# Loading pairs of KV-cache units as 2 MB transfers with 16 KB runs in a decode kernel

## The chip, the cores and the metric

The kernel runs on one core of one Trainium2 chip; the other cores are idle. The metric is the device time of one execution in microseconds (us), of which the profiled span is some 2 us less. One program differs from run to run (the kernel before gave 638.4 to 641.0 us in all sessions together), so each kernel is compared with runs of the kernel before from the same rounds, with an interval.

## The reference, cut to what matters

Two decoder layers, twice the same pair of blocks: attention of one new token against a KV cache, then a gated feed-forward block. Both layers use the same weights and the same caches.

```python
B, Sq, D = 4, 1, 512
Hq, Hkv, Sk, Dh = 32, 8, 8192, 128          # bf16 everywhere
def _A_ref(x, k_cache, v_cache, wq, wo):     # attention
    q = (x @ wq)...                          # 4 query heads share a KV head
    p = softmax(q k^T * Dh**-0.5);  o = p v
    return o @ wo
x = x + _A_ref(_layernorm(x), ...);  x = x + _B_ref(_layernorm(x), ...)   # layer 1
x = x + _A_ref(_layernorm(x), ...);  x = x + _B_ref(_layernorm(x), ...)   # layer 2
```

For each batch and KV head, K and V are 8192 rows of 256 bytes, 2 MB each: 4 x 8 x 2 x 2 MB = 128 MB a layer. Layer 2's query of a batch needs that batch's whole layer 1 first.

## The kernel before

PE is TensorE, PEld its weight load, DVE VectorE, ACT ScalarE, and SPq the queue of SyncE that issues the loads. The kernel streams the caches as *units* of 1 MB (half of one head's K or V), each into one of 11 *slots* of 8 KB per partition (15 once the query weights are no longer needed). A static *plan* simulates PE, DVE, ACT and the load queue and fixes the order of every instruction before the program is built; a list of tokens, ORDER, gives the order of the loads: `K` is the next key unit, `a061` layer 1's values of batch 0, head 6, half 1, `b...` the same for layer 2. A `c` token loads nothing: it is a value unit of layer 2 that has stayed in its slot since layer 1. The last unit is loaded in two halves, to shorten the tail. (A unit of 1 MB is 2^20 bytes; in lines of the profile and in the curves below, MB are 10^6 bytes.)

```python
class Plan:
    HOP = 0.06
    PAGE = 6.0          # us; the plan's own figure for PAGE_N instructions of PE
    PAGE_N = 256
    LOAD_LEAD = 2.1     # us; the plan's own figure, issue to first byte
    LOAD_TAIL = 1.7     # us; the plan's own figure, last byte to semaphore
...
def load_pair(u):
    kind, l, b, g, cp = u
    def fn():
        s = PL.slot[home[u]]
        cache = A_k_cache if kind == "k" else A_v_cache
        src = cache[b, g, cp * 2 * CR:(cp + 1) * 2 * CR, :].rearrange("(p t) d -> p (t d)", p=P)   # 1 MB, 8 KB per partition
        T.dma("sp", slot_sb(s), src, sem_slot[s], ...)      # waits until the slot's last reader is done
    return PL.load(2.495, fn, u)                            # 2.495 us in the plan; the last unit goes another way
...
def chain(b, deps, prior):                                  # from layer 1's attention of batch b to layer 2's query
    s = add_x(x0T[:], "x0", None, deps)
    opj_free[0] = s
    s = ffn(s, f"f{b}")
    cen, root = layer_norm(s, f"q{b}n")
    ...                                                     # query projection, spread over the key layout
k_order = [(g, cp) for cp in range(NCP) for g in range(G)]  # key units: half 0 of all heads, then half 1
```

Of the kernel before, what the change touches and what calls it, by code (L numbers as in the profile page):

```python
# [100 lines left out]


class Step:
    __slots__ = ("eng", "us", "deps", "fn", "prio", "take", "free", "start", "end", "slot_of", "n", "gives")

    def __init__(self, eng, us, fn, deps, prio, take=None, free=None, n=0):
        self.n = n
        self.eng, self.us, self.fn, self.prio = eng, us, fn, prio
        self.deps = [d for d in deps if d is not None]
        self.take, self.free = take, free  # L110
        self.start = self.end = None
        self.slot_of = None
        self.gives = 0


class Plan:

    HOP = 0.06
    PAGE = 6.0
    PAGE_N = 256  # L120
    LOAD_LEAD = 2.1
    LOAD_TAIL = 1.7

    def __init__(self, nslots, banks):
        self.steps = []
# [7 lines left out]
        self.steps.append(s)  # L133
        return s

    def load(self, us, fn, slots):
        s = Step("sp", us, fn, [], [0])
        s.slot_of = slots
        self.loads.append(s)
        return s  # L140

    def run(self):
# [19 lines left out]
        def finish(s):  # L162
            done.append(s)
            for u in users.get(s, ()):
                waits[u] -= 1
                if waits[u] == 0:
                    t = max(d.end + (self.HOP if d.eng != u.eng else 0.0) for d in u.deps)
                    todo[u.eng].append((t, u))

        def pump(now):  # L170
            nonlocal li, sp_at, dma_at
            while li < len(self.loads):
                s = self.loads[li]
                t = sp_at
                if s.slot_of is not None:
                    if not slots:
                        return
                    slots.sort()
                    f, i = slots[0]
                    t = max(t, f)  # L180
                    if t > now:
                        return
                    slots.pop(0)
                    self.slot[s.slot_of] = i
                s.start = t
                sp_at = t + 0.35
                dma_at = max(dma_at, t + self.LOAD_LEAD) + s.us
                s.end = dma_at + self.LOAD_TAIL
                li += 1
                finish(s)  # L190
# [18 lines left out]
        while left:  # L209
            best = None  # L210
            for e in engines:
                cand = None
                for t, s in todo[e]:
                    if s.take is not None:
                        b = min(bank_free.values()) if bank_free else None
                        if b is None:
                            continue
                        t = max(t, b)
                    at = max(t, free_at[e])
                    k = (at > free_at[e] + 1e-9, at if at > free_at[e] + 1e-9 else 0.0, s.prio[0])  # L220
                    if cand is None or k < cand[0]:
                        cand = (k, at, s)
                if cand is not None and (best is None or cand[1] < best[0]):
                    best = (cand[1], cand[2])
            nxt = None
            if li < len(self.loads) and (slots or self.loads[li].slot_of is None):
                nxt = max(sp_at, min(slots)[0] if self.loads[li].slot_of is not None else 0.0)
            if best is None and nxt is None:
                raise RuntimeError("the plan is stuck")
            if best is None or (nxt is not None and nxt <= best[0]):  # L230
                pump(nxt)
                continue
            at, s = best
            s.start, s.end = at, fetched(at, s)
            free_at[s.eng] = s.end
            for i, (_, x) in enumerate(todo[s.eng]):
                if x is s:
                    todo[s.eng].pop(i)
                    break
            if s.take is not None:  # L240
                b = min(bank_free, key=lambda x: bank_free[x])
                del bank_free[b]
                held[s.take] = b
                self.bank[s.take] = b
            if s.free is not None:
                bank_free[held.pop(s.free)] = s.end + self.HOP
            if s.slot_of is not None:
                slots.append((s.end + self.HOP, self.slot[s.slot_of]))
            for i in range(s.gives):
                slots.append((s.end + self.HOP, self.nslots + i))  # L250
            left -= 1
            finish(s)
# [4 lines left out]
    def emit(self):  # L257
        for s in sorted(self.steps + self.loads, key=lambda s: (s.start, s.prio[0])):
            s.fn()


ORDER = ("c100 c101 K K c260 x K c300 c301 c261 K wq K K wg1 c120 K K c340 K K K K c341 K a061 K K K wo1 a060 "
         "K K wo0 K K a010 K c240 K K a071 c121 a011 wg0 c031 K a070 a000 c370 K c371 a040 a001 K a050 K wu0 "
         "a030 c030 K a041 a051 K K K K a020 K a031 a021 a150 wo2 a151 a171 a170 wo3 wu1 wd0 wd1 a160 a161 "
         "a131 a130 K K K a121 K a110 a111 K K K K K K K K K K K b010 c241 a141 a120 b011 a140 a100 K K K K K "
         "b061 K K K K K K b060 a101 K b070 K K K b071 K c200 c201 b040 b041 b050 b051 b020 b001 b000 b021 K "
         "K K a250 c141 a251 K c140 K K K K K K K K K K K K a270 K a271 a220 a221 a210 a260 a201 K K K K K "
         "a240 K a200 a261 a241 K a230 K a231 K K a211 K b151 b150 K K b160 K b170 K b171 c321 b161 b110 b130 "
         "b131 b111 K a330 a310 K K a360 K K K K K K a361 K K a331 K K K K K a320 a350 a351 a311 a300 a370 "
         "a301 a341 a340 a321 a371 b230 b250 b231 b251 b220 b221 K K K K K K K K K K K K K K K K b210 b271 "  # L270
         "b270 b310 b211 b360 b320 b351 b311 b350 b331 b330 b361 ")
NSLOT = 11
NP = 2
NQB = 1
# [6 lines left out]
def bass_interleave_layers__gqa_block_cached__swiglu_ffn__decode_kernel(  # L281
# [18 lines left out]
    P = 128  # L300
# [14 lines left out]
    with ExitStack() as es:  # L315
# [230 lines left out]
        def slot_sb(s):  # L546
            return pool[:, s, :] if s < NSLOT else wq_sb[:, s - NSLOT, :]

        def load_pair(u):
            kind, l, b, g, cp = u  # L550

            def fn():
                s = PL.slot[home[u]]
                cache = A_k_cache if kind == "k" else A_v_cache
                src = cache[b, g, cp * 2 * CR:(cp + 1) * 2 * CR, :].rearrange("(p t) d -> p (t d)", p=P)
                T.dma("sp", slot_sb(s), src, sem_slot[s],
                      writes=[f"slot{s}_0", f"slot{s}_1"] + ([f"wq{s - NSLOT}"] if s >= NSLOT else []))
            home[u] = u
            if u != last_unit:
                return PL.load(2.495, fn, u)  # L560

            def half(h):
                s = PL.slot[home[u]]
                src = A_v_cache[b, g, cp * 2 * CR:(cp + 1) * 2 * CR, :].rearrange("(p h t) d -> p h (t d)", p=P, h=2)
                T.dma("sp", slot_sb(s)[:, h * UE:(h + 1) * UE], src[:, h, :], sem_half if h == 0 else sem_slot[s],
                      writes=[f"slot{s}_{h}"] + ([f"wq{s - NSLOT}"] if s >= NSLOT and h == 0 else []))
            return [PL.load(1.25, lambda: half(0), u), PL.load(1.25, lambda: half(1), None)]

# [333 lines left out]
            fs = slice(k * FO // 2, (k + 1) * FO // 2)  # L902
            wspec[f"wd{k}"] = (wd_sb[:, fs, :], B_w_down.rearrange("(fo p) n -> p fo n", p=P)[:, fs, :], 2.6)

        k_order = [(g, cp) for cp in range(NCP) for g in range(G)]
        k_order = [x for x in k_order if x[0] >= G // 2] + [x for x in k_order if x[0] < G // 2]

        def k_units(l, b):
# [10 lines left out]
        late_groups = [(1, B - 1, g) for g in LATE]  # L919
        last_unit = None  # L920
        if TAILSPLIT:
            last_unit = ("v", 1) + tuple(int(x) for x in [t for t in tokens if t[0] == "b"][-1][1:])

        w_load = {}
        loads = {}
# [1 line left out]
        ki = 0  # L927
        wq_load = None
        for npos, t in enumerate(tokens):
            if t == "K":  # L930
                u = kseq[ki]
                ki += 1
                prio[u] = [npos]
                if u[1] == 1 and ("k", 0) + u[2:] in kept_k:
                    home[u] = ("k", 0) + u[2:]
                else:
                    loads[u] = load_pair(u)
            elif t[0] in "abc":
                u = ("v", int(t[0] != "a")) + tuple(int(x) for x in t[1:])
                prio[u] = [npos]  # L940
                if t[0] == "c":
                    home[u] = ("v", 0) + u[2:]
                else:
                    loads[u] = load_pair(u)
            elif t == "x":
                x_load = PL.load(0.1, lambda: T.dma("sp", xrow, A_x.rearrange("b s d -> (b s) d"), sem_x,
                                                    writes=["xrow"]), None)
            elif t == "wq":
                wq_load = w_piece(wq_sb[:], A_wq.rearrange("(kt p) n -> p kt n", p=P), "wq", 9.94)
            else:  # L950
                w_load[t] = w_piece(*wspec[t][:2], t, wspec[t][2])
# [120 lines left out]
```

## Time and profile before

| | |
|---|---|
| time | 639.13 us (638.86 to 639.25, 3 runs) |
| span of the profile | 636.9 us |
| bytes loaded by queue 1 | 256.14 MB in 97.9% of the span |
| PE, DVE | 62%, 64% busy |

The prediction below shows the page's own lines. One more view belongs to it: what the issuing queue waits for (columns: who waited for whom; us in total, times, longest).

```profile
SPq L62 <- PE ps L601: 297.0, 112, 12.3
SPq L62 <- PE ps L742: 133.5, 67, 10.4
```

For two thirds of the span the issuer waits for PE to finish with a slot (L601 are the key matmuls, L742 the value matmuls). That is harmless as long as enough loads are already queued (queue 1 is busy for 97.9% of the span all the same).

### The profile page before, as it was taken

Reading aid. Unit: us, or ns where it says so; the run is one execution under the profiler, and the core shown is the slowest. Engines: PE = TensorE matmul, PEld = TensorE weight load, DVE = VectorE, ACT = ScalarE, POOL = GpSimd, SP = SyncE. Lnnn points to the kernel's source line nnn. Section 1 sums busy time; section 2 is a strip of 40 time slices with the busy share of each in tenths; the row PEclk is TensorE's granted clock in tenths of the full one; section 3 lists DMA queues with packets and bytes.
Section 4 is the critical chain, followed back from the end, with each engine's and each line's share of the span. In section 5 each row is a group of like instructions: output and inputs, shape, how many; then the busy total and the mean of one; then the engine's idle time right before and its main releaser. Section 6 shows DMA issues by size and latency. Waiting matters only on the chain.

```text
span 636.9 us, 18667 instructions
## 1 busy us (share of the span) xinstructions
PE 397.2 (62%) x8689; PEld 201.8 (32%) x8689; DVE 405.1 (64%) x615; ACT 40.4 (6%) x107; POOL 1.8 (0%) x8
## 2 busy tenths in 40 slices
PE   0375454365685556668577665668666676867576
PEld 0231221123552132235331241333421244621255
DVE  6386853464236958776578866457667863499832
ACT  1000200002000020000100100000100020000200
POOL 1000000000000000000000000000000000000000
PEclk9995586556557775655665687655566568576785
DMA  8999999999989999999999999999999999999991
GB/s 359 419 419 406 407 417 420 418 419 403 387 355 422 420 421 418 420 419 402 413 412 419 421 419 420 421 420 397 421 420 419 418 409 420 419 416 420 420 417 68
DMA packets 41125, 257.33 MB, mean 404 GB/s; under 512 B 3924, under 2 KB 9816, under 8 KB 11096
## 3 DMA queue, kind: packets, MB, share of 16 engines
q1 hardware_dynamic: 41048, 256.14, 97.9%
q8 instruction: 68, 1.11, 0.7%
q14 instruction: 9, 0.07, 0.0%
HBM read 256.12 MB, written 0.00 MB: 402 GB/s over the span
## 4 chain that ended last, share of the span: by engine, by line
DMA 66%; PE 15%; DVE 12%; SPq 3%; issue 2%
DMA pool<-in_A_k_cache_dram 44%; DMA pool<-in_A_v_cache_dram 13%; DVE pool L585 10%; PE ps L601 8%; DMA wq_sb<-in_A_v_cache_dram 5%; DMA wq_sb<-in_A_k_cache_dram 4%; PE ps L742 3%; SPq L92 3%; PE ps L463 1%; PE ps L788 1%; DVE wq_sb L585 1%; DVE ps L769 0%; PE ps L852 0%; PE ps L727 0%; PE ps L705 0%
## 5 line engine op out<-in xcount | busy, mean ns | idle before, releaser
L585 DVE STREAM_TRANSPOSE pool<-pool 128x2048 uint32<-128x2048 uint32 x116 | 266.9, 2308 | 91.3 <-DMA pool<-in_A_k_cache_dram 90.8
L601 PE MATMUL ps<-pool,qpad 32*32 32x512 bf16 x3840 | 193.2, 537 | 128.3 <-DVE pool L585 124.7
L601 PEld LDWEIGHTS ps<-pool,qpad 32*32 32x32 bf16 x3840 | 54.8, 108 | 243.9 <-DVE pool L585 184.4
L742 PE MATMUL ps<-pool,pp 128*32 128x256 bf16 x1936 | 98.8, 359 | 46.7 <-DMA pool<-in_A_v_cache_dram 36.5
L742 PEld LDWEIGHTS ps<-pool,pp 128*32 128x32 bf16 x1936 | 55.3, 118 | 82.8 <-DMA pool<-in_A_v_cache_dram 42.1
L769 DVE STREAM_TRANSPOSE ps<-ps 128x256 f32<-128x256 f32 x62 | 28.3, 457 | 60.9 <-PE ps L742 60.6
L624 ACT ACTIVATE pp<-ps,negm 128x512 bf16<-128x512 f32 x32 | 21.5, 685 | 322.3 <-DVE negm L620 299.8
L705 PE MATMUL ps<-oT,wo_sb 128*128 128x4 bf16 x640 | 22.6, 166 | 12.0 <-DVE oT L773 9.4
L705 PEld LDWEIGHTS ps<-oT,wo_sb 128*128 128x128 bf16 x640 | 20.2, 103 | 24.6 <-DVE oT L773 17.8
L620 DVE TENSOR_REDUCE negm<-ps 128x1 f32<-128x512 f32 x32 | 19.9, 683 | 11.6 <-PE ps L601 11.6
L463 PE MATMUL ps<-xnT,wq_sb 128*128 128x4 bf16 x640 | 18.3, 166 | 12.8 <-DMA wq_sb<-in_A_wq_dram 11.4
L463 PEld LDWEIGHTS ps<-xnT,wq_sb 128*128 128x128 bf16 x640 | 17.7, 104 | 15.2 <-DMA wq_sb<-in_A_wq_dram 11.6
L585 DVE STREAM_TRANSPOSE wq_sb<-wq_sb 128x2048 uint32<-128x2048 uint32 x8 | 18.5, 2311 | 1.3 <-DMA wq_sb<-in_A_k_cache_dram 1.3
L449 ACT ACTIVATE lnv<-var,eps_sb 128x4 f32<-128x4 f32 x10 | 3.0, 298 | 221.3 <-DVE var L444 221.3
L601 PE MATMUL ps<-wq_sb,qpad 32*32 32x512 bf16 x256 | 12.3, 512 | 7.4 <-DVE wq_sb L585 7.4
L660 PE MATMUL ps<-ident,pp 128*128 128x128 bf16 x128 | 15.8, 301 | 1.6 <-DVE oT L773 1.1
L660 PEld LDWEIGHTS ps<-ident,pp 128*128 128x128 bf16 x128 | 12.0, 138 | 9.1 <-DVE selw L680 2.9
L771 DVE TENSOR_REDUCE osum<-ps 128x4 f32<-128x32 f32 x62 | 11.9, 192 | 2.1
L773 DVE TENSOR_TENSOR oT<-osum,invL 128x4 bf16<-128x4 f32 x62 | 10.5, 169 | 2.1
L669 ACT ACTIVATE pp<-ps 128x1024 bf16<-128x1024 bf16 x8 | 8.2, 1023 | 29.7 <-PE ps L660 29.7
L671 DVE COPY pp<-ps 128x1024 bf16<-128x1024 bf16 x8 | 5.5, 690 | 6.8 <-PE ps L660 6.8
L649 DVE TENSOR_SCALAR pp<-pp,alpha 128x512 bf16<-128x512 bf16 x32 | 9.0, 344 | 1.1 <-ACT alpha L642 1.1
(68 smaller groups left out, 150.4 us busy)
## 6 DMA issues: line engine op xcount, KB each, us to landing
pool<-in_A_k_cache_dram SPq DMA_DIRECT2D x116, 1024.0 KB, 10.2
pool<-in_A_v_cache_dram SPq DMA_DIRECT2D x101, 1024.0 KB, 10.7
wq_sb<-in_A_k_cache_dram SPq DMA_DIRECT2D x8, 1024.0 KB, 14.8
wq_sb<-in_A_v_cache_dram SPq DMA_DIRECT2D x5, 1024.0 KB, 16.3
wq_sb<-in_A_wq_dram SPq DMA_DIRECT2D x1, 4096.0 KB, 20.1
wo_sb<-in_A_wo_dram SPq DMA_DIRECT2D x4, 1024.0 KB, 15.2
wg_sb<-in_B_w_gate_dram SPq DMA_DIRECT2D x2, 896.0 KB, 19.2
wu_sb<-in_B_w_up_dram SPq DMA_DIRECT2D x2, 896.0 KB, 16.9
```

Source lines behind the costliest of these rows:

```text
L92: ins = self.eng[engname].dma_start(out_ap, in_ap)
L463: op("pe", lambda e: e.matmul(ps[:, bk * BW + h * B:bk * BW + (h + 1) * B], lhsT=wq_sb[:, kt, h * Dh:(h + 1) * Dh], rhs=xnT[:, kt * B:(kt ...
L585: op("dve", lambda e: e.transpose(v, v), reads=keys, writes=keys)
L601: op("pe", lambda e: e.matmul(ps[32 * c:32 * (c + 1), a * BW:(a + 1) * BW], lhsT=qpad[rows, qbuf, es_, g, :], rhs=ap[h][rows, :, es_ // 2, ...
L620: op("dve", lambda e: e.tensor_reduce(negm[:, q, a:a + 1], bank(a), AX.X, ALU.max, negate=True), reads=[f"pb{a}"], writes=[f"negm{q}_{a}"])
L624: op("act", lambda e: e.activation(pblk(q)[:, :, a, :], bank(a).rearrange("p (t j) -> p t j", j=32), ACTF.Exp, bias=negm[:, q, a:a + 1], s ...
L660: op("pe", lambda e: e.matmul(stg[:, t * P:(t + 1) * P], lhsT=pp[:, q, blk * P:(blk + 1) * P], rhs=ident[:], is_transpose=True, start=True ...
L705: op("pe", lambda e: e.matmul(ps[:, OPJ * BW + nq * B:OPJ * BW + (nq + 1) * B], lhsT=wo_sb[:, h, nq * P:(nq + 1) * P], rhs=oT[:, l, h, :], ...
L742: op("pe", lambda e: e.matmul(ps[32 * n:32 * (n + 1), bk * BW:bk * BW + 256], lhsT=pp[:, q, col:col + 32], rhs=v[:, 8 * f:8 * (f + 1), 32 ...
L769: op("dve", lambda e: e.transpose(blk, blk), reads=[f"pb{bk}"], writes=[f"pb{bk}"])
L771: op("dve", lambda e: e.tensor_reduce(osum[:], diag, AX.X, ALU.add), reads=[f"pb{bk}"], writes=["osum"])
L773: op("dve", lambda e: e.tensor_tensor(oT[:, l, g * REP:(g + 1) * REP, b], got, invL[:, q, g * REP:(g + 1) * REP], ALU.mult), reads=[f"pb{b ...
```

## The change

The intent: fewer, longer packets. Each partition now holds 64 adjacent rows of a head's cache (16 KB) instead of two separate runs of 32, so that both units of a head can come as one 2 MB load of 16 KB runs into two adjacent slots. 27 pairs are loaded so (tokens `P`, `A..`, `B..`); the other units are still singles, which now read 8 KB out of every 16 KB. The plan's constants change too, and the order of the keys.

```diff
-    PAGE = 6.0
+    PAGE = 5.0
-    LOAD_TAIL = 1.7
+    LOAD_TAIL = 2.1
...
+        def rows_of(u):
+            cache = A_k_cache if u[0] == "k" else A_v_cache
+            return cache[u[2], u[3], :, :].rearrange("(p c t) d -> p c (t d)", p=P, c=NCP)
+
+        def load_two(u0, u1):
+            def fn():
+                s = PL.slot[u0]
+                to = pool[:, s:s + 2, :] if s < NSLOT else wq_sb[:, s - NSLOT:s - NSLOT + 2, :]
+                T.dma("sp", to.rearrange("p c e -> p (c e)"), rows_of(u0).rearrange("p c e -> p (c e)"), sem_slot[s], ...)
...
+            return PL.load(4.914, fn, u0, u1)
...
-                src = cache[b, g, cp * 2 * CR:(cp + 1) * 2 * CR, :].rearrange("(p t) d -> p (t d)", p=P)
-                T.dma("sp", slot_sb(s), src, sem_slot[s],
+                T.dma("sp", slot_sb(s), rows_of(u)[:, cp, :], sem_slot[s],
...
-                return PL.load(2.495, fn, u)
+                return PL.load(2.505, fn, u)
...
-        k_order = [(g, cp) for cp in range(NCP) for g in range(G)]
+        k_order = [(g, cp) for g in range(G) for cp in range(NCP)]
... (the scheduler learns to wait for two adjacent free slots; ORDER gets 16 P, 7 A and 4 B tokens)
```

## The prediction

> **What bounds the kernel now.** I read the page first, for the engine shares, the slices and the DMA queues.
>
> ```profile
> PE 397.2 (62%) x8689; PEld 201.8 (32%) x8689; DVE 405.1 (64%) x615; ACT 40.4 (6%) x107; POOL 1.8 (0%) x8
> DMA  8999999999989999999999999999999999999991
> GB/s 359 419 419 406 407 417 420 418 419 403 387 355 422 420 421 418 420 419 402 413 412 419 421 419 420 421 420 397 421 420 419 418 409 420 419 416 420 420 417 68
> DMA packets 41125, 257.33 MB, mean 404 GB/s; under 512 B 3924, under 2 KB 9816, under 8 KB 11096
> q1 hardware_dynamic: 41048, 256.14, 97.9%
> q8 instruction: 68, 1.11, 0.7%
> DMA 66%; PE 15%; DVE 12%; SPq 3%; issue 2%
> ```
>
> No compute engine is busy for two thirds of the span, while queue 1 is busy for 97.9% of it and moves about 420 GB/s in most slices. The last line, from the chain that ended last, agrees: 66% of it is DMA. So the kernel lasts as long as 256.14 MB take, plus a start, a tail, and the places where the queue runs dry. Those I looked for with the windows view in stretches of 5 us (columns: stretch, length, busy time and count of PE, PEld, DVE, ACT, POOL, then clock, DMA share, GB/s), and with the timeline of the issuing queue.
>
> ```profile
> 180.00:185.00 5.00, 3.99 (x158) 3.65 (x163) 0.91 (x5) 0.31 (x2) 0.00 (x0) 0.50 1.01 418
> 185.00:190.00 5.00, 4.58 (x108) 1.92 (x93) 3.30 (x5) 0.00 (x0) 0.00 (x0) 0.69 0.62 223
> 190.00:195.00 5.00, 3.60 (x138) 2.28 (x135) 0.00 (x0) 0.00 (x0) 0.00 (x0) 1.00 1.01 421
> ...
> 620.00:625.00 5.00, 1.87 (x67) 1.77 (x64) 0.83 (x3) 0.00 (x0) 0.00 (x0) 0.50 0.69 283
> 625.00:630.00 5.00, 3.77 (x114) 3.47 (x112) 1.28 (x8) 0.00 (x0) 0.00 (x0) 0.50 0.04 10
> ```
>
> ```profile
> 177.52 10.20 SPq L92 DMA_DIRECT2D pool<-in_A_v_cache_dram  x2
> 188.35 10.90 SPq L92 DMA_DIRECT2D pool<-in_A_k_cache_dram  x9
> ```
>
> The one real dry spell is at 185 to 190: 223 instead of 420 GB/s loses (1 - 223/420) x 5 = 2.3 us. The timeline says why: between the two loads of the group that begins at 177.52 and the nine of 188.35 the issuer sat for some 10 us, because the slots are full of layer 2's keys, which cannot be used before layer 2's query of batch 0 (its projection runs at 179.56 to 183.6 in the chain). Other soft stretches lose less: 393 and 385 at 285 to 295 are 0.3 + 0.4 us, 395 at 325 is 0.3, 380 at 435 is 0.5. The slices with 403, 387 and the rest of the loss in 355 (slices 10 to 12) hold the weights in 1 KB and 3.5 KB runs, not a wait. After the stream has ended near 625 a tail of about 12 us runs on PE and DVE: last value group, output projection, feed-forward.
>
> [...] its packet records give a median of 159 ns for 4096 B and 312 ns for 8192 B (most frequent 309), so 4096 B more cost 150 to 153 ns, 26.8 to 27.3 bytes per ns. [...] In this trace the overhead is what is left at zero size: 159 - 150 = 9 ns; 1024 B take 46 to 48 ns, of which 38 at that rate are data, again 8 to 10 ns. Completion packets of 4 B take 9 ns. [...] The pitch here goes from 8 to 16 KB; no run here shows what that does yet. [...] The 68 instruction packets of 16 KB take a median of 1073 ns beside the stream, where 16 KB alone should take about 610, so they do share; they also show that the trace records 16 KB as one packet.
>
> **The change part by part.** (a) *Bytes: none.* The order before has 235 units of 1 MB to place, less 4 kept keys, so 231 loads (116 + 8 + 101 + 5 whole, and one in two halves). After it are 177 singles and 27 pairs, 177 + 54 = 231; the list of kept values is the same 21. (b) *Packets.* A single is 8 packets of 8 KB on each engine and a completion: 8 x 312 + 9 = 2505 ns. A pair is 8 packets of 16 KB and one completion. My estimate of a 16 KB packet is 2 x (312 - 9) + 9 = 615 ns, so the pair takes 8 x 615 + 9 = 4929 ns against 2 x 2505 = 5010. Saved: 0.081 us a pair, 27 x 0.081 = 2.2 us in all. The constants in the plan (4.914 for a pair, 2.505 for a single) would say 27 x 0.096 = 2.6 us; they are what the author believes, and near mine. As the queue never pauses over most of the span, this should reach the end nearly whole; it also moves the query of batch 0 forward, since that waits for loads in front of it. (c) *Issue.* 27 issues fewer of about 0.35 us, but the queue works at least 10 us ahead (median of issue to landing 10.2 us), so this is worth 0. (d) *Singles with a hole.* The 177 singles now read 8 KB out of every 16 KB. Packets keep their size, so I expect 2.505 us still: 0. (e) *Pairs wait for two adjacent slots and land as one.* 14 of the 27 are in the first 63 MB, when slots come free in order; the others stand in a few stretches (149 to 164 MB and the last 35). The first unit of a pair becomes usable up to 2.4 us later; with some 4 MB always in flight the engines have work meanwhile: 0 to +0.5 us. (f) *New order of loads.* The search had new constants (page time 5, landing tail 2.1). Around the dry spell the tokens are nearly the same as before, with again 11 keys in a row before b010, so I expect most of its 2.3 us to stay: -0.5 us on average. (g) *Tail.* The pair B33 now stands before the last value load; before, its two units did, one of them landing about 2.5 us before the end (its matmuls start at 623.74 and run without a gap). The pair lands in the same place, so the tail stays at 12 us: 0.
>
> Sum: 639.1 - 2.2 (packets) - 0.5 (order) + 0.2 (pairing waits) = 636.6 us.
>
> **The rivals.** *Holes hurt.* If half-covered 16 KB blocks cost the memory something, say 1% of a single (0.025 us), the 177 singles lose 4.4 us and the time goes to 641. [...] Against it: the other half mostly follows within a few loads and the packets are the same. *Two adjacent slots turn into dry spells.* One more spell such as that at 185 costs 2.3 us, so 639; two, 641. For it: the issuer already waits for slots most of the span. Against it: the median 10 us in flight cover most waits, and the plan was made for them. *The new order removes the dry spells.* All of them together are about 4 us; with half gone the time is 634.5, with all near 632.7. Against it: that at 185 hangs on a chain of results, not on packets. [...] *The transfer was at its ceiling anyway*, by reads and not by packets: then (b) gives 0 and the time is 638.5 to 639.
>
> **Range and chances.** The sure part is small, 2.2 us or 0.35%; schedule luck is of the same size, about 2 us each way, and the holes add some weight above. I take 636.6 us, 633.0 to 640.5. Faster by 2% means below 626.3; that is more than the packets and every dry spell together (639.1 - 2.2 - 4 = 632.9), so 2%. Slower by 2% means above 651.9, a loss of over 2.8% on each single, or five more dry spells: 3%. Within 2%: 95%.
>
> **What would show it.** Right: packets fall by 27 x 128 in data and 27 x 16 in completions, to about 41125 - 3888 = 37240; 16 KB packets near 615 ns, 8 KB ones still at 312; clean slices that hold pairs at 425 or so against 420; bytes the same; the dry spell still near 183 to 187; a tail of about 12 us. Wrong: 8 KB packets longer than 314 ns (holes), 16 KB packets at 624 or more (no overhead to save), new stretches under 400 GB/s away from the weights (slots), or the stretch at 185 back at 420 (order).

"Its packet records" are those of the trace of before. Three figures are estimates from the trace of before: the 610 ns of 16 KB alone is 4 x 150 + 9, the 2.4 us of (e) is 4.929 - 2.505, and its 4 MB are 10.2 us at 420 GB/s. The 1% of "holes hurt" is a supposition; nothing measured stood behind it.

## The result, and the profile after

The changed kernel takes 639.02 us (median of 4, 638.6 to 640.06), the kernel before 639.19 us in the same rounds; the ratio is 0.9997, with a 95% interval of 0.998 to 1.0015. (A ratio is the mean time of one kernel's runs over that of the other's in the same rounds, so not quite the ratio of the medians.) The same program ran once more by accident, as x_pair8k below: 0.9989. Together that is 0.2 to 0.7 us of gain instead of the 2.5 us forecast, within noise of nothing.

The page of the changed kernel, the same lines as shown of before:

```profile
PE 397.1 (62%) x8689; PEld 205.1 (32%) x8689; DVE 402.7 (63%) x615; ACT 40.4 (6%) x107; POOL 1.8 (0%) x8
DMA  8999999999989999999999999999999999999991
GB/s 356 423 426 412 405 417 423 420 418 401 387 348 400 422 418 419 420 412 421 402 408 419 422 425 428 417 408 420 418 408 421 415 419 421 417 409 419 423 425 65
DMA packets 37237, 257.32 MB, mean 404 GB/s; under 512 B 3492, under 2 KB 9384, under 8 KB 10664
q1 hardware_dynamic: 37160, 256.14, 97.7%
q8 instruction: 68, 1.11, 0.7%
DMA 63%; PE 18%; DVE 16%; issue 2%; SPq 0%; ACT 0%
```

The packets fell to 37237 as worked out, the bytes are the same, and some slices run at 423 to 428 GB/s. But the busy share of queue 1 fell as well, from 97.9 to 97.7% of a span that is no shorter: time that the packets no longer need has become idle time. Slices 12 and 13 (348, 400; before 355, 422) show where. The windows of the changed kernel there, and at the end, then its issuing queue at the spell:

```profile
185.00:190.00 5.00, 4.02 (x80) 1.69 (x79) 3.13 (x4) 0.00 (x0) 0.00 (x0) 0.50 0.62 215
190.00:195.00 5.00, 4.49 (x160) 2.63 (x144) 0.00 (x0) 0.00 (x0) 0.00 (x0) 0.91 0.96 339
620.00:625.00 5.00, 2.08 (x76) 1.78 (x73) 0.83 (x3) 0.00 (x0) 0.00 (x0) 0.94 0.66 270
625.00:630.00 5.00, 3.78 (x114) 3.48 (x112) 1.28 (x8) 0.00 (x0) 0.00 (x0) 0.50 0.03 9
```

```profile
176.69 10.76 SPq L92 DMA_DIRECT2D pool<-in_A_v_cache_dram  x2
188.13 7.07 SPq L92 DMA_DIRECT2D pool<-in_A_k_cache_dram  x8
```

The dry spell is still at 185 to 190 (215 GB/s, before 223) and goes on into the next stretch, 339 GB/s where before had 421. The issuer stops at 176.69 us, 0.83 us sooner than before (177.52), but goes on with keys at 188.13, only 0.22 us sooner (188.35). The end of the stream is at the same place.

The packet records of the trace give the sizes. The median 16 KB packet took 614 ns (estimate 615), the median 8 KB packet 311 ns (312). All packets of queue 1 together, over 16 engines, come to 622.2 us in the changed kernel and 622.5 in its repetition, against 623.6 and 624.0 in the two profiles of before: about 1.5 us less.

To find where these were lost, I took from the same records the moment by which a given number of MB had been moved. Every kernel here moves the same MB in all, so the difference of two such curves is the time one is ahead. Negative is ahead of the first profile of before:

| | at 75 MB (before: 184.9 us) | at 85 MB (211.1 us) | at 255 MB (620.8 us) |
|---|---|---|---|
| changed kernel | -0.60 | +0.55 | 0.00 |
| the same, repeated (x_pair8k) | -0.79 | +0.80 | -0.19 |

All 14 pairs ahead of the spell are loaded before 66 MB (13 of them before 55), and by 75 MB the changed kernel is 0.6 to 0.8 us ahead. It loses all of it and more within the ten MB that hold the dry spell. From there to the end it wins back 0.5 to 1.0 us.

### The profile page after: what moved, and what is told of

Read it like the earlier page. It is cut to its first block, busy times and chain, and to the rows that moved or that the text cites. A ratio compares the mean times of both kernels' runs of the same rounds, so it can differ in the third digit from the quotient of the medians.

```text
span 636.9 us, 18609 instructions
## 1 busy us (share of the span) xinstructions
PE 397.1 (62%) x8689; PEld 205.1 (32%) x8689; DVE 402.7 (63%) x615; ACT 40.4 (6%) x107; POOL 1.8 (0%) x8
## 2 busy tenths in 40 slices
DMA packets 37237, 257.32 MB, mean 404 GB/s; under 512 B 3492, under 2 KB 9384, under 8 KB 10664
## 3 DMA queue, kind: packets, MB, share of 16 engines
q1 hardware_dynamic: 37160, 256.14, 97.7%
## 4 chain that ended last, share of the span: by engine, by line
DMA 63%; PE 18%; DVE 16%; issue 2%; SPq 0%; ACT 0%
DMA pool<-in_A_k_cache_dram 39%; DMA pool<-in_A_v_cache_dram 18%; DVE pool L606 12%; PE ps L622 7%; PE ps L763 5%; DMA wq_sb<-in_A_wq_dram 3%; PE ps L472 2%; DMA wo_sb<-in_A_wo_dram 2%; DMA wq_sb<-in_A_k_cache_dram 2%; DVE wq_sb L606 1%; PE ps L809 1%; PE ps L726 1%; DVE ps L790 1%; PE ps L681 1%; PE ps L873 1%
## 5 line engine op out<-in xcount | busy, mean ns | idle before, releaser
L622 PE MATMUL ps<-pool,qpad 32*32 32x512 bf16 x3840 | 190.6, 543 | 127.2 <-DVE pool L606 120.7
L763 PEld LDWEIGHTS ps<-pool,pp 128*32 128x32 bf16 x1936 | 57.5, 122 | 81.6 <-DMA pool<-in_A_v_cache_dram 42.8
L472 PE MATMUL ps<-xnT,wq_sb 128*128 128x4 bf16 x640 | 18.3, 166 | 12.1 <-DMA wq_sb<-in_A_wq_dram 11.4
L438 PE MATMUL ps<-xx,onesm 128*128 128x32 f32 x20 | 6.3, 410 | 5.3 <-DVE xx L433 4.3
```

The costliest lines, as they stand in the source:

```text
L472: op("pe", lambda e: e.matmul(ps[:, bk * BW + h * B:bk * BW + (h + 1) * B], lhsT=wq_sb[:, kt, h * Dh:(h + 1) * Dh], rhs=xnT[:, kt * B:(kt ...
L622: op("pe", lambda e: e.matmul(ps[32 * c:32 * (c + 1), a * BW:(a + 1) * BW], lhsT=qpad[rows, qbuf, es_, g, :], rhs=ap[h][rows, :, es_ // 2, ...
L763: op("pe", lambda e: e.matmul(ps[32 * n:32 * (n + 1), bk * BW:bk * BW + 256], lhsT=pp[:, q, col:col + 32], rhs=v[:, 8 * f:8 * (f + 1), 32 ...
```

## The experiments

15 runs. In the tables of "ahead" the numbers are as above.

### The packets by themselves: s_seq, s_hole, s_pair

A program of nothing but loads: 256 MB of the caches into ten slots, no compute.

```diff
 s_seq:  src = [head[c * 4096:(c + 1) * 4096, :].rearrange("(p t) d -> p (t d)", p=P) for c in range(2)]
 s_hole: src = [head.rearrange("(p c t) d -> p c (t d)", p=P, c=2)[:, c, :] for c in range(2)]
 s_pair: src = [head.rearrange("(p t) d -> p (t d)", p=P)]        # two slots at once
```

> The disputed cost by itself: nothing but loads, all 128 MB of K and V caches twice (256 loads of 1 MB), contiguous 1 MB halves as in the kernel before, ten slots, no compute (the result is wrong on purpose). From the packet records of before, a load is 8 x 312 + 9 = 2.505 us, so 256 take 641 us, about 646 us with start and end. Theory (packets cost 9 ns each, holes cost nothing) and its rivals agree on this run; it is the base for the next two.

> The same stream of 1 MB loads, but each load reads 8 KB out of every 16 KB, as the changed kernel's singles do (wrong result on purpose). Theory: equal to s_seq within 1 us, 8 KB packets at a median of 311 to 312 ns. Rival 'holes hurt': 1% or more slower (6 us), 8 KB packets at 315 ns or more.

> The same bytes as 128 loads of 2 MB in 16 KB runs (wrong result on purpose). Theory: a pair is 8 x 614 + 9 = 4.921 us against 5.010, so 128 x 0.089 = 11.4 us less than s_seq (about 1.8%). Rival 'the transfer was at its ceiling anyway': equal to s_seq within 2 us.

Measured: 644.44, 645.05 and 634.0 us (one run each, spans 642.6, 643.2 and 632.2). The pages of s_seq, s_hole and s_pair, in this order:

```profile
DMA packets 36898, 268.47 MB, mean 418 GB/s; under 512 B 4128, under 2 KB 4128, under 8 KB 4128
```

```profile
DMA packets 36898, 268.47 MB, mean 417 GB/s; under 512 B 4128, under 2 KB 4128, under 8 KB 4128
```

```profile
DMA packets 18465, 268.46 MB, mean 425 GB/s; under 512 B 2080, under 2 KB 2080, under 8 KB 2080
```

The pairs save 10.44 us in 128, 0.082 us each, the estimate to within a hundredth (mean 16 KB packet 615.5 ns, mean 8 KB packet 313.8). The holes cost 0.6 us in 256 loads, one run each, and the curves of the two streams stay within 0.12 us of each other. So the packet step of the prediction was right, and "the transfer was at its ceiling anyway" and "holes hurt" are both wrong for a bare stream. (The saving of 11.4 us expected of s_pair was 1 us too high.)

### An attempt that said nothing: x_pair8k

```diff
-T.dma("sp", to.rearrange("p c e -> p (c e)"), rows_of(u0).rearrange("p c e -> p (c e)"), sem_slot[s],
+T.dma("sp", to, rows_of(u0), sem_slot[s],
```

> The changed kernel with the same 27 pairs in the same order, each still one 2 MB load with one completion, but its runs are 8 KB (the two slots are written as separate pieces): 27 x 128 more packets, nothing else. Theory (the packet saving is real, but some of it is lost where the queue is dry anyhow): 0.7 to 2.0 us slower than the changed kernel, so 639.7 to 641, ratio to before 1.001 to 1.003. Rival 'packets are worth nothing here': equal to the changed kernel, ratio 1.000. Note that if the pair is still cut into 16 KB packets the run says nothing; the packet count will show it (40693 or so, against 37237).

It took 638.97 us, ratio 0.9989 (0.9977 to 1.0001). Its page has the packets of the changed kernel and not the 40693 wanted:

```profile
DMA packets 37237, 257.32 MB, mean 404 GB/s; under 512 B 3492, under 2 KB 9384, under 8 KB 10664
```

The two adjacent pieces were loaded as runs of 16 KB again (the record does not show what merged them). The run is therefore a repetition of the changed kernel and is used as that; it tells nothing of packets.

### The parts of the change alone: x_consts, x_korder, x_holes, x_nopairs, and before_again

x_consts is before with `PAGE = 5.0`, `LOAD_TAIL = 2.1` and 2.505 us per single. x_korder adds the new `k_order`. x_nopairs is the changed kernel with the ORDER of before (constants, holes and key order, no pairs); x_holes is that with the key order of before. The plan gives all four the same schedule: their traces have the same instructions in the same order on every engine. All four load in the ORDER of before, so none of them tests the new order.

> The kernel before with only the plan's constants of the change (page time 5, landing tail 2.1, single load 2.505), its own order of loads, no pairs, contiguous halves. It separates what the other schedule costs from what the pairs bring. Theory A (the change's gain from pairs was spent by its schedule): 1 to 2 us slower than before, ratio 1.0015 to 1.003. Theory B (the pairs never brought the gain inside this kernel): equal to before within 0.5 us.

> x_consts with the key units in the change's order (both halves of a head one after the other), contiguous halves, no pairs. x_nopairs was 1.3 us slower than x_consts; it differs by this order and by the holes. If the order of the keys does it: ratio 1.002 or more (640.7). If not: as x_consts, 1.000 (639.4).

> x_nopairs with the key units in the order of before: holes and constants alone. The bare streams say that holes cost under 0.6 us in 256 loads. If they are as cheap here: 639.4 to 640.0, ratio 1.000 to 1.001. If the holes made x_nopairs slow: 640.7 or more, 1.002.

> The changed kernel with the order of loads of before, so no pairs: its layout (64 adjacent rows per partition, singles with holes) and its constants alone. The static schedule of the engines is the same as in x_consts, only the rows that a load brings differ. Theory: equal to x_consts within 0.5 us. Rival 'holes hurt': 231 loads slower by 1% each, 5.8 us more than x_consts. If theory A of x_consts holds, the changed kernel is 1 to 2 us faster than this one.

> The kernel before once more, unchanged: it shows how far two sets of runs of one program differ, and a second profile of the dry spell near 185. In the first profile of before the TensorE clock came back from half to full at 188.1, in all four kernels of the other schedules only at 190.8 to 191.6, so that their slots came free about 1.2 us later. Theory 'luck of the clock': the step to full speed lies anywhere between 187 and 192 in this profile too, and if it is late the dry stretch is as long as in the changed kernel. Theory 'schedule': it lies at 188 again. Ratio 1.000.

| | median us | ratio to before (95%) | ahead at 75, 85, 255 MB |
|---|---|---|---|
| before_again | 639.27 | 0.9998 (0.9986 to 1.001) | -0.08, +0.37, +0.37 |
| x_consts | 639.62 | 1.0003 (0.999 to 1.0016) | -0.14, +0.34, +0.98 |
| x_korder | 639.64 | 1.0003 (0.9991 to 1.0015) | -0.05, +0.42, +1.37 |
| x_holes | 639.90 | 1.0008 (0.9995 to 1.0021) | 0.00, +0.41, +0.62 |
| x_nopairs | 640.89 | 1.0024 (1.0012 to 1.0037) | +0.15, +0.98, +2.21 |

Only x_nopairs is clear of noise, at +1.5 us. Neither of its two layout parts alone shows that, and the bare stream clears the holes, but no run repeats both parts together, so whether its excess over x_holes is chance stays open. x_consts has the time of theory B (equal to before) and not of A (1 to 2 us slower), though its interval reaches A's lower end. What the four have in common is that behind the dry spell they lose 0.2 to 1.2 us (85 to 255 MB, mean 0.8), which the two profiles of before do not, and their ratios average 1.0010, 0.6 us. So the new constants, with the old order of loads, are perhaps half a microsecond worse than the old ones; each single run is too coarse to say more.

before_again also answers its own question in part: the clock came back to full at 189.0 there, against 188.1 in the first profile and 190.8 to 191.6 in the changed kernel, its repetition, the four above and x_early below. It varies within one program, but whether the later step of these seven is chance or schedule stays open. The constants alone do not fix it: the last two kernels below have them too, and there it came at 187.4 and 192.4.

### Only the pairs ahead of the spell: x_early

The tokens of the last 13 pairs are taken apart, for example `A20` into `a200 a201`, `P` into `K K`.

> The changed kernel with only its first 14 pairs (those before the dry spell); the other 13 are taken apart into two singles at the same place. Theory 'the spell swallows what was gained before it': these 14 bring nothing, the time is that of x_nopairs, 640.9, and the changed kernel's gain over x_nopairs comes from the late 13. Theory 'the gain passes through the spell, since the chain that ends it begins with loads': 14 x 0.08 = 1.1 us less, 639.8, half way to the changed kernel.

It took 639.77 us, ratio 1.0011 (0.9998 to 1.0024): 0.3 us under the mean ratio of the two kernels with the layout and no pairs (1.0008 and 1.0024) and 1.2 us over the changed kernel's (0.9993, mean of its two). The median is what the second theory, "the gain passes", had forecast (639.8), while the ratio, a mean that one run of 641.47 us pulls up, lies between the two; the intervals overlap, so the time decides nothing. Its trace is plainer: ahead by 0.41 at 75 MB and behind by 0.70 at 85 MB (and by 2.08 at 255 MB: without the late pairs it loses another 1.4 us there). All three kernels with early pairs come to the spell 0.4 to 0.8 us ahead and leave it 0.55 to 0.80 behind; the four without pairs that share their constants come at -0.14 to +0.15 and leave at +0.34 to +0.98. **The spell puts them level.** These are single executions, but all seven agree.

### Why the spell does not end sooner

The spell ends when PE frees the slots held by layer 1's four kept key units, which needs layer 2's query of batch 0. PE in the timeline there, before, then changed (columns: start and length in us, engine, line, operation, tiles, count, idle time just before and what ended it):

```profile
184.81 1.05 PE L601 MATMUL ps<-pool,qpad 32*32 32x512 bf16 x16
186.28 1.05 PE L601 MATMUL ps<-pool,qpad 32*32 32x512 bf16 x16 [0.42 <-issue]
...
188.62 1.12 PE L601 MATMUL ps<-pool,qpad 32*32 32x512 bf16 x32
```

```profile
183.98 1.05 PE L622 MATMUL ps<-pool,qpad 32*32 32x512 bf16 x16
186.01 1.05 PE L622 MATMUL ps<-pool,qpad 32*32 32x512 bf16 x16 [0.98 <-issue]
...
188.82 1.91 PE L622 MATMUL ps<-pool,qpad 32*32 32x512 bf16 x32
```

The pairs do bring the query forward, as predicted: the first half unit starts at 183.98 instead of 184.81, 0.83 us sooner. But the second half starts only 0.27 us sooner, because PE stands idle for 0.98 us instead of 0.42 and waits there for nothing that the profile shows ("issue"). In the three profiles with these early pairs the first half starts at 183.98 to 184.07 and the second at 186.01 to 186.21; in the six without, at 184.76 to 185.02 and 186.14 to 186.69. Of a mean lead of 0.85 us, 0.38 is left.

That the wait is for further instructions is inferred, from three numbers. The trace has 68 instruction packets of 16 KB, and PE and PEld have 2 x 8689 instructions, 255.6 to the packet. One of these packets runs from 183.7 to 184.8 in before and from 183.4 to 184.5 in the changed kernel. And PE resumes 1.25 to 1.5 us after the end of such a packet in each of the nine profiles. No run varies the instructions alone, so the cause is not shown.

The third line of each fence shows a second cause, which does not belong to the change by its design: the next 32 matmuls take 1.91 us instead of 1.12, at a granted clock of 0.50 (mean of 188.8 to 190.7 us), where before had 1.00 from 188.1 us on. The windows around it, before, then changed:

```profile
187.00:191.00 4.00, 4.00 (x120) 2.28 (x120) 2.57 (x4) 0.00 (x0) 0.00 (x0) 0.87 0.73 262
```

```profile
187.00:191.00 4.00, 4.00 (x85) 1.88 (x78) 1.75 (x4) 0.00 (x0) 0.00 (x0) 0.52 0.75 254
```

PE is busy for the whole 4 us in both, but has done 120 matmuls in one and 85 in the other, at a mean clock of 0.87 and 0.52. In both traces the steps of the clock lie multiples of 3.41 us apart (188.1, 198.3, 205.1 in before), and in two runs of one program (the changed kernel and x_pair8k) the same step came at 190.9 and 191.6. What decides them no run shows.

### The spell taken away: x_short_before, x_short_none, x_short_after26

The feed-forward of batch 0 is left out of the chain to layer 2's query (a wrong computation):

```diff
-            s = ffn(s, f"f{b}")
+            if b > 0:
+                s = ffn(s, f"f{b}")
```

x_short_before is before with this. x_short_after26 is the changed kernel with it, and one `P` (some 150 MB into the loads) taken apart; x_short_none is that with all its pairs taken apart.

> The kernel before with the feed-forward left out of the chain that leads to layer 2's query of batch 0 (wrong result on purpose): that query is ready some 9 us sooner, so the dry spell at 185 to 190 us, 2.3 us long, should vanish. Both theories expect about 636.8 us, 2.3 less than before. It is the base for x_short_after26.

> The changed kernel with the same cut in the chain of batch 0 (wrong result on purpose), and one pair of keys (the one some 150 MB into the loads) taken apart into two singles, because with the shorter chain that pair would find no two adjacent slots for some 7 us. 26 pairs remain. If the dry spell near 185 swallowed the gain of the pairs before it (3.4 us lost there after the change against 2.4 before), this one gains 3.4 us over the changed kernel and is 1.0 to 1.5 us faster than x_short_before: 635.4 to 635.8. If the gain is missing for another reason, it equals x_short_before within 0.5 us.

> x_short_after26 with its 26 pairs taken apart into singles at the same places: layout, constants, order and the cut chain of batch 0 stay (wrong result on purpose). No dry spell near 185 in either. If pairs bring their whole 26 x 0.08 = 2.1 us where nothing swallows it, this is 2.1 us slower than x_short_after26: 637.7, ratio about 0.9975, as x_short_before. If layout and constants eat it, this is slower than x_short_before too, by 1 us or more: 638.7.

The windows at the place of the spell, x_short_before, then x_short_after26:

```profile
185.00:195.00 10.00, 4.29 (x80) 1.93 (x80) 3.14 (x4) 0.00 (x0) 0.00 (x0) 0.66 1.01 419
```

```profile
185.00:195.00 10.00, 3.92 (x80) 1.80 (x80) 4.08 (x5) 0.00 (x0) 0.00 (x0) 0.79 1.02 422
```

The spell is gone in both. The times:

| | median us | ratio to before (95%) | ahead at 75, 85, 255 MB |
|---|---|---|---|
| x_short_before | 637.75 | 0.9978 (0.9966 to 0.9991) | -0.03, -2.33, -1.02 |
| x_short_none | 637.52 | 0.9967 (0.9955 to 0.9979) | +0.02, -2.28, -0.99 |
| x_short_after26 | 635.55 | 0.9941 (0.9927 to 0.9954) | -0.57, -2.88, -2.39 |

Now the lead of the early pairs, 0.59 us at 75 MB over x_short_none, passes 85 MB undiminished (2.88 - 2.28 = 0.60), and the late ones add 0.8 us (2.39 - 0.99 = 1.40 in all). By time the 26 pairs are worth (0.9967 - 0.9941) x 639.6 = 1.7 us, with an interval of about 1.1 us either way, against 26 x 0.082 = 2.1. And x_short_none, which has the new order with its pairs taken apart, is not slower than x_short_before, so here neither layout, constants nor order eat anything. Two expectations missed: x_short_after26 was 2.2 us faster than x_short_before and not 1.0 to 1.5, and x_short_before gained 1.4 us and not 2.3, because it lost 1.3 us of it again behind the spell, mostly between 95 and 115 MB.

### More pairs: x_best12, x_best13

If a pair is worth 0.08 us wherever the queue is the bound, there should be more of them. A random search over ORDER, with the plan's own model and constants and nothing else changed, found orders with 67 and 68 pairs and the same bytes. Only the ORDER text differs; that of x_best12:

```text
c030 P x c260 wq P c101 P P P wu0 P P P A05 P P wg0 c240 wo2 K wg1 A06 c340 K K K A00 P P P wo3 c120 A04 A01 P K A02 A03
wo1 A07 A17 wo0 wu1 A16 K A15 c261 K wd1 c300 K wd0 A13 P K K K K P P c341 P P A11 c241 c121 c141 P B01 P B06 A10 A12 P P
A14 K K c200 b070 K K K b071 K b041 c031 b040 b050 b020 b051 B00 c370 b021 K K c371 c140 K K K K a210 K c301 K K K K K K
K K a220 K a221 a211 A27 P K A26 K P P P A25 P P A20 K A23 A24 B16 K B11 b151 b150 b170 B13 b171 c201 K K c100 K K K K K
K K K a310 K K K A33 K K a350 K a311 c321 a351 A36 A34 a321 A30 a320 a370 a371 b230 b231 b220 b221 b250 K K K K P P K K
K K K K K K B27 b210 b251 b211 B33 b320 B35 B31 b360 b361
```

> The changed kernel with another order of loads (found by a search with the plan's own constants): 67 pairs instead of 27, 97 singles, same bytes, same layout, correct result. 40 more pairs x 0.08 = 3.3 us off the packets. The dry spell near 185 stays (and the pairs before it should again bring little). Theory: pairs before the spell (about 30 of the 67) are swallowed in good part, the 37 behind it count: 639.0 less 2 to 3.3 us, 635.7 to 637.0, ratio 0.995 to 0.9965. Rival 'more pairs only make more waits for two adjacent slots': 639 or more.

> A second order from the same search, 68 pairs, with fewer planned waits behind the spell (0.64 us at one place instead of 1.7 us at three) but a longer planned tail. Theory: as x_best12 within 1 us, 635.7 to 637.0. Rival: 639 or more.

x_best12 took 635.70 us (635.36 to 637.98) with a correct result, ratio 0.9948 (0.9932 to 0.9963), 3.3 us faster than before and faster than the changed kernel. x_best13 took 636.91 us, 0.996 (0.994 to 0.9979). The page of x_best12, and its windows at the spell:

```profile
DMA packets 31476, 257.31 MB, mean 406 GB/s; under 512 B 2852, under 2 KB 8744, under 8 KB 10024
```

```profile
185.00:190.00 5.00, 4.83 (x176) 3.07 (x181) 4.93 (x3) 0.00 (x0) 0.00 (x0) 0.76 0.67 234
190.00:195.00 5.00, 1.15 (x59) 0.61 (x39) 4.93 (x6) 0.00 (x0) 0.00 (x0) 0.92 0.98 374
```

Its spell is still there (234, 374), and takes its toll: 1.82 us ahead at 75 MB, 0.64 at 85 MB, 1.88 at 255 MB. The packets sum to 618.9 us, 4.9 less than the mean of before's two profiles, and the profiled span is 3.3 us shorter. But 1.4 us of these 3.3 come after 255 MB: the stream's last MB takes less time (it ends at 622.97 us against 625.70, 2.7 sooner) and the tail behind it, in which nothing is loaded, is 0.6 us shorter. x_best13, with one pair more, loses its lead at the spell altogether (1.76 us ahead at 75 MB, 0.22 behind at 85 MB, 0.32 ahead at 255 MB); its clock came back at 192.4 us, that of x_best12 at 187.4. Neither order was run with its pairs taken apart, so how much of their gain is due to the pairs and how much to the order is not shown.

## Why the prediction was wrong

- *(a) bytes and (b) packets, their size:* right. 37237 packets were counted against 37240 or so, 614 ns against 615, and 0.082 us a pair in the bare stream against 0.081.
- *(b) "this should reach the end nearly whole; it also moves the query of batch 0 forward":* **the step that failed.** The query did move forward, by 0.83 us. But the dry spell's end does not move with it: the chain behind the query is PE's, with 0.98 us of idle time, probably (not shown) for instructions, and matmuls at half clock (0.50): of 0.83 us of lead at the query's first matmuls, 0.27 are left at the next and 0.22 when the loads go on. In all three profiles with these early pairs the 0.4 to 0.8 us gained by 75 MB had become a lag of 0.55 to 0.80 by 85 MB. So about half of the 27 pairs, those ahead of the spell, brought close to nothing; with the spell taken away, the 0.6 us that they had gained passed. (14 x 0.082 would be 1.15 us. Between 57 and 60 MB all four kernels with these pairs lose 0.2 to 0.5 us of it; no run shows why.)
- *(d) holes:* right. The bare stream shows 0.6 us in 256 loads, one run each.
- *(e) two adjacent slots:* not isolated by a run. In the plan it is a real danger (with the cut chain one pair would have waited some 7 us for two adjacent slots, which is why I took it apart), but the changed kernel's trace shows no sign of it: behind the spell seven stretches of 5 us are under 400 GB/s (387 to 398), where before has four, but its repetition has four as well.
- *(f) order, -0.5 us:* not shown either way. That most of the dry spell stays was right. But the new order ran without pairs only where the spell was cut away (x_short_none: ratio 0.9967 against 0.9978, intervals overlapping); the four kernels with the new constants and the old order average 0.6 us slower than before, though only one of them by more than its interval.
- *(g) tail:* right. At 255 MB the changed kernel and its repetition are 0.0 to 0.2 us ahead, and from the last load to the end it is 11.2 us before and after.
- *A reading:* the issuer's wait of some 10 us lies between the two loads of the group at 177.52 (177.52 and 187.39 us), not behind them. It changes nothing in the argument.

Put together, as an estimate: the early half of the pairs about 0, the late 13 about -1.1 (13 x 0.082), the schedule perhaps +0.6 (measured with the old order alone), so -0.5 us, and 0.2 to 0.7 us of gain were measured. That packets become shorter was right; the step from packets to time was not: 2.2 us of packets were booked as 2.2 us of time. Of the rivals, none was this one as written. Two had the number, by luck: "at its ceiling anyway" (638.5 to 639), which s_pair refutes, and "one more spell" (639), of which the trace shows nothing. The nearest sentence was against "the new order removes the dry spells": that the spell hangs on a chain of results and not on packets. It should have been turned round: what hangs on a chain need not get faster with packets (here 0.22 of 0.83 us were left).

What stays open: how much of the later clock step in the seven profiles with the new constants is chance, which waits make up the 0.2 to 1.4 us that the kernels with the new constants and no late pairs lose behind the spell, and what the new order does by itself.

## What to carry to other kernels

When a stream is "98% busy" but runs dry at one place because of a chain of results, a saving in the stream counts only for the part behind that place (and ahead of it only as far as the chain's end moves with it; here 0.60 us ahead at 75 MB became 0.55 behind at 85 MB); draw the curve of bytes moved against time for both kernels and see where the lead dies. Longer runs per partition paid here even above 8 KB (16 KB runs took a pure stream from 644.44 to 634.0 us, 1.6%), but take enough of them, and put them where nothing else sets the pace: 27 pairs gave nothing measurable; 67 pairs together with another order gave 0.5%.

## Figures of the hardware that these runs gave

- Packets: their cost at zero size is about 9 ns, worked out from 159 ns for 4096 B and 309 ns (the most frequent) for 8192 B in before; its 4 B packets took 9. Going from 8 KB to 16 KB runs took a bare stream from 644.44 to 634.0 us.
- Holes: 8 KB runs at a pitch of 16 KB cost 0.6 us in 644 us (645.05 against 644.44), one run each.
- Instruction packets: one of 16 KB beside the load stream took a median of 1073 ns in before and 1075 in the changed kernel, whose 16 KB packets of loads took 614. At the end of 62 of the 68 in before an 8 KB packet of a load began that took 764 to 856 ns (median 801) instead of 312. PE idled 0.33 to 1.13 us at one place (inferred to be a wait for instructions) in nine profiles.
- Clock: PE was at half clock (0.50) for 41 us (147 to 188 us of before) with matmuls in flight for 28.3 us of it. Which share of busy time would have ended that, no run shows.
- End of the stream: half of the packets in flight are gone some 3 us before the rest. In the kernel before, 16 were in flight until 621.5 us, 8 or 9 from 622.75 to 624.75 (the records do not name their engines); in the bare stream s_seq, the drop from 16 to 1 took about 1 us.
